# A list scheduler that counts a port shared by VectorE and GpSimd, and lets either take the low parts of weights

## The chip, the cores and the metric

The kernel runs on one core of one Trainium2 chip. The metric is device time in microseconds (us) for one execution, as the median of several; lower is better.

## The reference

A decay attention over 2 batches, 8 heads, 768 positions of width 64 feeds two feed-forward layers. The batch and head dimensions of its output are laid out as 1536 tokens by 512, and then:

```python
g = x @ w_gate                          # 512 x 1536
silu = g * (1.0 / (1.0 + np.exp(-g)))
val = x @ w_val
y = silu * val @ w_out                  # 1536 x 512: first MLP
h = y @ w_in                            # 512 x 2048
out = (h * np.cos(h)) @ w_out2          # 2048 x 512: second MLP
```

All weights come as 64-bit floats and are read as pairs of 32-bit words.

## The kernel before

Every large product is made of three fp32r matmuls (`mm3`, lines 142 to 147): high part of the weight by low part of the data, high by high, low by high. So every operand needs a high part (a copy on ScalarE) and a low part (a subtraction). One token block of 512 is a bank of the PSUM memory; eight banks circulate. Two of the three token blocks go through a seven-product scheme (products `b c a d 2 3 4`) that needs sums of weight pieces (`sa`, `sb` in the first MLP, `ta`, `tb` in the second) and of data pieces (the tiles `t1`, `t2`, `t3`).

The attention stage comes first (its code and order are not touched), with six first-MLP products in its last chunks. After it, all remaining work is given out by a list scheduler that runs while the kernel is built. Jobs are Python generators: each yields requests for an engine with a length in ns, or takes and gives buffers (`stock`: `s`, `g`, `y`, `ct`, `stage`, `ring`, `bank`). `run_all` picks what starts next by the lengths it believes in, emits the instruction, and so fixes one order for each engine. On the chip the engines keep that order and wait for each other by semaphores.

The jobs that matter here:

- `conv_job` turns one loaded weight piece into fp32: a scaling on ScalarE (`scale`, L189, tile `ct`), a shift (`shift`, L194, tile `raw`) and a merge (`join`, L201, `ct`) on VectorE. `split_job` then makes the high part `wh` on ScalarE and the low part `wl` on GpSimd (L638).
- `sums_job` makes two weight sums from two `ct` tiles in four half-size operations (128x256) on GpSimd.
- `turn_job` computes h*cos(h): ScalarE rounds, VectorE subtracts multiples of 2 pi twice (L921, tile `y`; L923, tile `s`), ScalarE takes absolute value and sine, VectorE multiplies. `finish` splits the result into `gh` (ScalarE) and `gl` (VectorE).
- `t_job` and `y_job` prepare `t1` to `t3` for the first and the second MLP with 128x1024 operations on VectorE; the tile they work in is named `sum`, their high parts go through ScalarE.
- `copy_job` copies product `b` or `c` from its bank to an `s` tile on ScalarE. Product `d` adds onto the bank of `c` and waits for that copy.
- `flush_job` adds a finished bank to a running `sum` on VectorE.

The scheduler's lengths for a 128x512 operation are 604 ns on VectorE and 1254 ns on GpSimd, whatever the other engine does. Data tiles in the "small" part of the weight ring are given up in `ring_down`, which makes room for the `s`, `g` and `y` tiles of the second MLP.

Of the kernel before, what the change touches and what calls it, by code (L numbers as in the profile page):

```python
# [45 lines left out]
def kernel(  # L46
# [463 lines left out]
    pieces = sorted(first_use, key=first_use.get)  # L510
    loads = [p for p in pieces if p[0] not in ("sa", "sb", "ta", "tb")]
    turned = min(seen[op] for op in downs[first2:]) - TURN

    mlp, live, ts, sums, where = {}, {}, {}, {}, {}
    f32 = lambda x: tuple(t.bitcast(F32) for t in x)
# [45 lines left out]
        "ct": [(0, i) for i in range(CT)], "stage": [], "ring": [],  # L561
    }
    wanted = {pool: [] for pool in stock}
    free_at = dict.fromkeys(("PE", "ACT", "DVE", "POOL"), 0)
    waiting = {e: [] for e in ("ACT", "DVE", "POOL")}
    n_jobs = [0]
    pe_units, pe_downs = [], []
# [59 lines left out]
        wanted[pool].remove(e)  # L627
        resume(e[2], t, i)

    def go(engine, ns, fn):  # L630

        return engine, ns, fn

    def tt(out, in0, in1, op, engine="DVE"):

        unit = nc.vector if engine == "DVE" else nc.gpsimd
        n = math.prod(out.shape[1:])
        return go(engine, n * (1.18 if engine == "DVE" else 2.45), lambda: unit.tensor_tensor(out=out, in0=in0, in1=in1, op=op))  # L638

    def act(out, src, fn, **kw):  # L640

# [3 lines left out]
    def either(out, in0, in1, op):  # L645

        n = math.prod(out.shape[1:])
        return "any", {"DVE": n * 1.18, "POOL": n * 2.45}, lambda e: (nc.vector if e == "DVE" else nc.gpsimd).tensor_tensor(
            out=out, in0=in0, in1=in1, op=op)

    def allowed(e, job, req):

# [2 lines left out]
    def run_all():  # L655

        while True:
            best = None
            for e in waiting:
                asks = [x for x in waiting[e] if allowed(e, *x)]  # L660
                if asks:
                    start = max(free_at[e], min(job.t for job, _ in asks))
                    if best is None or start < best[0]:
                        best = start, e
            op = next_pe()
            if op and (best is None or op[0] < best[0]):
                start, sub = op
                free_at["PE"] = start + sub["n"] * 227
                run_pe(sub, free_at["PE"])
                continue  # L670
            if best is None:
                assert not pe_units and not pe_downs and not blocked, (pe_units[:1], pe_downs[:1], blocked, wanted)
                return
            start, e = best
            job, req = min((x for x in waiting[e] if x[0].t <= start and allowed(e, *x)), key=lambda x: (x[0].prio, x[0].n))
            ns = req[1]
            if req[0] == "any":
                ns = ns[e]
                waiting["DVE"].remove((job, req))
                waiting["POOL"].remove((job, req))  # L680
                req[2](e)
            else:
                waiting[e].remove((job, req))
                req[2]()
            free_at[e] = start + ns
            resume(job, start + ns + LATENCY)

    unit_banks = set()
# [65 lines left out]

    def ring_job():

        for key in pieces[n_conv[0]:]:
            eligible = last_use[key] < turned
            if key[0] in ("sa", "ta"):
                other = ("sb" if key[0] == "sa" else "tb", key[1])  # L760
                got = []
                for k in (key, other):
                    i = yield "take", "ring", last_use[k] < turned
                    c = yield "take", "ct"
                    got.append((k, i, c))
                spawn(sums_job(got), first_use[key] - AHEAD, (yield "now",))
            elif key[0] not in ("sb", "tb"):
                yield "wait", ("load", key)
                i = yield "take", "ring", eligible
                c = yield "take", "ct"  # L770
                spawn(conv_job(key, i, c), first_use[key] - AHEAD, (yield "now",))
            granted.add(key)

    def split_job(key, i):

        wh, wl = ring_tiles(key, i)
        where[key] = i
        yield act(wh, fp[key], AF.Copy)
        yield tt(wl, fp[key], wh.bitcast(F32), ALU.subtract, "POOL")
        wsp[key] = (wh, wl)  # L780

    def conv_job(key, i, c):

        yield go("ACT", 550, lambda: scale(key, c))
        yield go("DVE", 455, lambda: shift(key))
        yield go("DVE", 610, lambda: join(key))
        now = yield "now",
        give("stage", stage_of.pop(key), now)
        signal(("fp", key), now)
        yield from split_job(key, i)  # L790
        now = yield "now",
        signal(("w", key), now)
        if key not in unsummed:
            give("ct", c, now)
        else:
            ct_of[key] = c

    def sums_job(got):

        which, f = got[0][0]  # L800
        rows = (("gate", f), ("val", f)) if which == "sa" else (("in2", f), ("in2", f + 1))
        for row in rows:
            yield "wait", ("fp", row)
        (a11, a12), (a21, a22) = ([fp[row][:, h * 256:h * 256 + 256] for h in range(2)] for row in rows)
        s = []
        for key, i, c in got:
            t = fp[key] = word_tile(c)
            s += [t[:, 0:256], t[:, 256:512]]
        yield tt(s[0], a21, a22, ALU.add, "POOL")
        yield tt(s[1], s[0], a11, ALU.subtract, "POOL")  # L810
        yield tt(s[2], a11, a21, ALU.subtract, "POOL")
        yield tt(s[3], a12, s[1], ALU.subtract, "POOL")
        for row in rows:
            unsummed.discard(row)
        for key, i, c in got:
            spawn(sum_split_job(key, i, c), first_use[key] - AHEAD, (yield "now",))
        for row in rows:
            yield "wait", ("w", row)
            if row in ct_of:
                give("ct", ct_of.pop(row), (yield "now",))  # L820
# [4 lines left out]
        signal(("w", key), (yield "now",))  # L825
        give("ct", c, (yield "now",))

    stage_of, ct_of, granted, last_load = {}, {}, set(), [0]
    unsummed = {(nm, f) for nm in ("gate", "val") for f in range(GROUP1, NF1)} | {("in2", f) for f in range(NF2)}

    def ring_down(t):

        small = range(RINGS[0], sum(RINGS[:2]))
        if "small" not in mlp or any(last_use[key] < turned and key not in granted for key in pieces[n_conv[0]:]):
            return
        if any(i in small for i in where.values()) or sum(i in small for _, i in stock["ring"]) < RINGS[1]:
            return
# [35 lines left out]
    def val_job(key, b, ps):  # L873

        yield "wait", ("s",) + key
        i, s = live.pop(key)
        yield tt(s, s, ps, ALU.mult)
        drop_bank(b, (yield "now",))
        yield from finish(key, i, s)

# [11 lines left out]
    def add_job(kind, f, nm, ps):  # L892
# [1 line left out]
        src, key = {"a": ("b", (0, f)), "2": ("d", (1, f)), "3": ("c", (1, f + (kind == "r")))}[nm]  # L894
        yield "wait", (kind, f, src)
        i, s = live[kind, f, src]
        yield tt(s, ps, s, ALU.add)
        signal((kind, f, nm), (yield "now",))
        key = ((0, 1)[kind == "r"],) + key
        if kind == "r":  # L900
            spawn(turn_job(key, s, lambda t: give("s", i, t)), seen[key] - EARLY, (yield "now",))
        elif nm != "3":
            yield act(s, s, AF.Silu)
            live[key] = i, s
# [5 lines left out]
            give("s", i, (yield "now",))  # L910
            yield from finish(key, j, s0)

    def turn_job(key, up, release):

        i = yield "take", "s"
        s = s_tile(i)
        n_ = s.bitcast(I32)
        yield act(n_, up, AF.Copy, scale=1.0 / (2.0 * math.pi))
        k = yield "take", "y"
        y = y_tile(k)  # L920
        yield go("DVE", 710, lambda: nc.vector.scalar_tensor_tensor(  # L921
            out=y, in0=n_, scalar=-TWO_PI_1, in1=up, op0=ALU.mult, op1=ALU.add))
        yield go("DVE", 610, lambda: nc.vector.scalar_tensor_tensor(  # L923
            out=s, in0=n_, scalar=-TWO_PI_2, in1=y, op0=ALU.mult, op1=ALU.add))
        give("y", k, (yield "now",))
        yield act(s, s, AF.Abs)
        yield go("ACT", 629, lambda: nc.scalar.activation(s, s, AF.Sin, scale=-1.0, bias=halfpi))
        yield tt(s, s, up, ALU.mult)
        release((yield "now",))
        yield from finish(key, i, s)  # L930

    def up_sub(op):
# [10 lines left out]
        def then(t):  # L943
            b, ps = held
            if nm == "in2":
                spawn(turn_job(key, ps, lambda t: drop_bank(b, t)), seen[key] - EARLY, t)
            else:
                spawn((gate_job if nm == "gate" else val_job)(key, b, ps), seen[op], t)
            if op == ("val", 1, GROUP1 - 1):
# [5 lines left out]
    def product_sub(op):  # L955
# [28 lines left out]
        def then(t):  # L984
# [4 lines left out]
            else:  # L989
# [2 lines left out]
                    spawn(val_job((0, 0, f), b, ps), seen[op], t)  # L992
                else:
                    key = (1, 0, f + 1)
                    spawn(turn_job(key, ps, lambda t: drop_bank(b, t)), seen[key] - EARLY, t)
            if kind == "q" and nm == "4" and f == NF1 - 1:
                signal("plain2", t)

# [39 lines left out]
    def flush_job(ph, blk, i, i_):  # L1038
# [10 lines left out]
        if first:  # L1049
            yield act(sm, ps, AF.Copy)  # L1050
        else:
            yield tt(sm, ps, sm, ALU.add)
        now = yield "now",
        give("bank", b, now)
        if last and ph == 0:
# [59 lines left out]
    with tc.manual_schedule():  # L1115
# [62 lines left out]
        stock["ct"] = [(0, i) for i in range(CT) if i not in ct_of.values()]  # L1178
        grow(1, mlp["small"])
        stock["ring"] = [(0, i) for i in free[n_conv[0]:]]  # L1180
        ahead = loads[n_conv[0]:n_loaded[0]]
        for n, key in enumerate(loads[:n_loaded[0]]):
            if key in ahead:
# [43 lines left out]
```

## Time and profile before

| | |
|---|---|
| median of 3 runs | 636.59 us (636.31 to 638.22) |
| the profiled execution, its own time | 636.19 us |
| its span, first to last instruction | 634.4 us |
| TensorE matmuls | 604.6 us busy, 95% of the span |
| VectorE | 475.7 us, 75% |
| ScalarE | 330.8 us, 52% |
| GpSimd | 248.1 us, 39% |
| DMA, mean over the span | 77 GB/s from and to HBM |

A busy share is a mean over stages that differ: the attention stage ends near 80 us, the first MLP near 380 us, and the second MLP takes the rest. Matmuls overlap in the pipeline, so that TensorE's own rate is read from the distance between the starts of two matmuls and not from the length of one.

### The profile page before, as it was taken

To read this page: it belongs to the slowest core of one execution; us is meant where nothing else is said; L and a number is where in the kernel's file an instruction comes from. 1 tells how busy PE (TensorE), PEld (TensorE's weight loads), DVE (VectorE), ACT (ScalarE), POOL (GpSimd) and SP (SyncE) were. 2 spreads that over 40 slices of the span, in tenths; PEclk is the share of its full clock that TensorE was granted. 3 is DMA by queue.
4 is the path that set the end of the run, shared out by engine and by line. 5 is a ranking of instruction groups with operands and counts; after the bars stand their busy time and mean duration, and the time that the engine had idled before them with its cause. 6 is when DMAs were issued, how large, how long until landed. Compare 5 with 4: busy or idle time off the path is not lost.

```text
span 634.4 us, 8339 instructions
## 1 busy us (share of the span) xinstructions
PE 604.6 (95%) x3093; PEld 490.3 (77%) x3093; DVE 475.7 (75%) x664; ACT 330.8 (52%) x570; POOL 248.1 (39%) x212
## 2 busy tenths in 40 slices
PE   8999999599999999999999989899889999999997
PEld 5888878477888887788888867688668788878886
DVE  4676569975545457665477899899998999998854
ACT  2353435556462534443532568787667575756630
POOL 3333356973544343442522136116342535161000
PEclk9999999799999999999999999799999999999999
DMA  9998222331221131122231012122312131100005
GB/s 186 210 247 191 67 68 69 125 105 43 92 67 66 39 95 66 68 67 63 72 100 33 1 53 80 33 68 66 101 33 91 42 92 42 67 1 1 0 2 199
DMA packets 65433, 49.31 MB, mean 78 GB/s; under 512 B 38760, under 2 KB 60272, under 8 KB 65392
## 3 DMA queue, kind: packets, MB, share of 16 engines
q1 hardware_dynamic: 65360, 48.77, 27.2%
q8 instruction: 24, 0.39, 0.3%
q14 instruction: 17, 0.14, 0.1%
q10 hardware_dynamic: 32, 0.01, 0.0%
HBM read 45.61 MB, written 3.15 MB: 77 GB/s over the span
## 4 chain that ended last, share of the span: by engine, by line
PE 58%; DVE 26%; issue 5%; ACT 5%; POOL 4%; DMA 1%; DVEq 0%; POOLq 0%; ACTq 0%
PE bank L145 13%; PE bank L146 12%; PE bank L147 12%; PE bank L1020 4%; PE bank L1019 4%; PE bank L1021 4%; DVE sum L638 4%; DVE s L638 4%; DVE s L923 4%; DVE gl L638 4%; DVE ct L201 3%; DVE y L921 3%; DVE raw L194 2%; POOL ct L638 2%; PE bank L406 2%
## 5 line engine op out<-in xcount | busy, mean ns | idle before, releaser
L638 POOL TENSOR_TENSOR wl<-ct,wh 128x512 fp32r<-128x512 f32 x98 | 147.4, 1516 | 256.6 <-ACT wh L643 213.1
L145 PE MATMUL bank<-xl,wh 128*128 128x512 f32 x336 | 134.1, 399 | 14.7 <-ACT s L643 8.9
L146 PE MATMUL bank<-xh,wh 128*128 128x512 f32 x336 | 132.0, 393 | 0.0
L147 PE MATMUL bank<-xh,wl 128*128 128x512 f32 x336 | 131.8, 392 | 0.0
L638 DVE TENSOR_TENSOR gl<-s,gh 128x512 fp32r<-128x512 f32 x81 | 71.5, 885 | 45.0 <-ACT gh L643 44.8
L643 ACT ACTIVATE wh<-ct 128x512 fp32r<-128x512 f32 x98 | 59.6, 627 | 64.5 <-DVE ct L201 53.2
L145 PEld LDWEIGHTS bank<-xl,wh 128*128 128x128 f32 x336 | 63.6, 189 | 33.7 <-ACT s L643 10.9
L643 ACT ACTIVATE s<-s 128x512 f32<-128x512 f32 (+1 forms) x92 | 57.5, 629 | 59.6 <-DVE s L923 32.1
L145 PE MATMUL bank<-wl,gh 128*128 128x512 f32 x192 | 75.6, 394 | 2.2 <-DVE sum L638 2.0
L643 ACT ACTIVATE gh<-s 128x512 fp32r<-128x512 f32 x81 | 50.5, 626 | 49.0 <-PE bank L1020 36.6
L638 DVE TENSOR_TENSOR sum<-bank,sum 128x512 f32<-128x512 f32 x100 | 64.7, 682 | 14.8 <-PE bank L147 7.7
L147 PE MATMUL bank<-wh,gl 128*128 128x512 f32 x192 | 75.2, 392 | 0.0
L146 PE MATMUL bank<-wh,gh 128*128 128x512 f32 x192 | 75.2, 392 | 0.0
L147 PEld LDWEIGHTS bank<-xh,wl 128*128 128x128 f32 x336 | 63.6, 189 | 13.5
L146 PEld LDWEIGHTS bank<-xh,wh 128*128 128x128 f32 x336 | 63.7, 190 | 12.4
L638 POOL TENSOR_TENSOR ct<-ct 128x256 f32<-128x256 f32 x72 | 69.7, 987 | 3.3 <-DVE ct L201 2.0
L643 ACT ACTIVATE s<-bank 128x512 f32<-128x512 f32 (+1 forms) x91 | 53.2, 588 | 28.8 <-PE bank L147 27.7
L201 DVE SCALAR_TENSOR_TENSOR ct<-ct,raw 128x512 int32<-128x512 int32 x68 | 56.2, 826 | 7.3 <-ACT ct L189 4.9
L1019 PE MATMUL bank<-gh,wl 128*128 128x512 f32 x144 | 56.1, 389 | 0.0
L638 DVE TENSOR_TENSOR s<-bank,s 128x512 f32<-128x512 f32 x54 | 36.9, 684 | 25.5 <-PE bank L147 24.1
L1021 PE MATMUL bank<-gl,wh 128*128 128x512 f32 x144 | 56.0, 389 | 0.0
L1020 PE MATMUL bank<-gh,wh 128*128 128x512 f32 x144 | 56.0, 389 | 0.0
(99 smaller groups left out, 946.0 us busy)
## 6 DMA issues: line engine op xcount, KB each, us to landing
raw<-in_moe_w_out_dram SPq DMA_DIRECT2D x28, 512.0 KB, 3.3
raw<-in_moe_w_in_dram SPq DMA_DIRECT2D x16, 512.0 KB, 3.8
raw<-in_moe_w_gate_dram SPq DMA_DIRECT2D x12, 512.0 KB, 3.5
raw<-in_moe_w_val_dram SPq DMA_DIRECT2D x12, 512.0 KB, 3.5
q<-in_q_dram SPq DMA_DIRECT2D x12, 256.0 KB, 4.9
k<-in_k_dram SPq DMA_DIRECT2D x12, 256.0 KB, 5.1
v<-in_v_dram SPq DMA_DIRECT2D x12, 256.0 KB, 5.9
out_dram<-sum SPq DMA_DIRECT2D x12, 256.0 KB, 2.1
```

Of the source, the lines that this page charges most:

```text
L145: nc.tensor.matmul(ps, wh, xl, start=first, stop=False, **kw)
L146: nc.tensor.matmul(ps, wh, xh, start=False, stop=False, **kw)
L147: nc.tensor.matmul(ps, wl, xh, start=False, stop=last, **kw)
L194: nc.vector.tensor_scalar(out=lo, in0=lo, scalar1=29, scalar2=None, op0=ALU.logical_shift_right)
L201: nc.vector.scalar_tensor_tensor(out=w, in0=w, scalar=3, in1=lo, op0=ALU.logical_shift_left, op1=ALU.bitwise_or)
L638: return go(engine, n * (1.18 if engine == "DVE" else 2.45), lambda: unit.tensor_tensor(out=out, in0=in0, in1=in1, op=op))
L643: return go("ACT", 40 + n * 0.94, lambda: nc.scalar.activation(out, src, fn, **kw))
L921: yield go("DVE", 710, lambda: nc.vector.scalar_tensor_tensor(out=y, in0=n_, scalar=-TWO_PI_1, in1=up, op0=ALU.mult, op1=ALU.add))
L923: yield go("DVE", 610, lambda: nc.vector.scalar_tensor_tensor(out=s, in0=n_, scalar=-TWO_PI_2, in1=y, op0=ALU.mult, op1=ALU.add))
L1019: nc.tensor.matmul(ps, lo[:, cs], gh, start=first, stop=False)
L1020: nc.tensor.matmul(ps, hi[:, cs], gh, start=False, stop=False)
L1021: nc.tensor.matmul(ps, hi[:, cs], gl, start=False, stop=last)
```

## The change

In the scheduler, a VectorE operation whose operands all lie in SBUF and any operation of GpSimd now hold one shared resource, `port`, for the length that the scheduler believes in; one that reads PSUM does not. The low parts of weights (`wl`) and the sums of weights, which went to GpSimd, become requests of kind `either`: VectorE may always take one, GpSimd only where VectorE is so long in its present instruction that GpSimd would end earlier. A request's earliest start is computed for each one apart, then priority decides. ScalarE, VectorE and GpSimd are taken to be free only some us after the start of the scheduled part; banks carry times at which they come free. The small ring tiles are used for a prefix of the pieces, so that they can be given up by count.

```diff
+    n_small = next(n for n, key in enumerate(pieces) if last_use[key] >= turned)
...
-    free_at = dict.fromkeys(("PE", "ACT", "DVE", "POOL"), 0)
+    free_at = {"PE": 0, "ACT": 2400, "DVE": 1800, "POOL": 4000, "port": 0}
...
-    def go(engine, ns, fn):
-        return engine, ns, fn
+    def go(engine, ns, fn, port=False):
+        return engine, ns, fn, port or engine == "POOL"
...
-                asks = [x for x in waiting[e] if allowed(e, *x)]
-                if asks:
-                    start = max(free_at[e], min(job.t for job, _ in asks))
-                    if best is None or start < best[0]:
-                        best = start, e
+                for job, req in waiting[e]:
+                    if not allowed(e, job, req):
+                        continue
+                    start = max(free_at[e], job.t, free_at["port"] if req[3] else 0)
+                    rank = max(start, free_at[e]), job.prio, job.n
+                    if best is None or rank < best[0]:
+                        best = rank, e, job, req
...
             free_at[e] = start + ns
+            if req[3]:
+                free_at["port"] = start + ns
...
-            eligible = last_use[key] < turned
+            eligible = n < n_small
...
-            granted.add(key)
+            granted[0] = n + 1
+            ring_down((yield "now",))
...
-        yield tt(wl, fp[key], wh.bitcast(F32), ALU.subtract, "POOL")
+        yield either(wl, fp[key], wh.bitcast(F32), ALU.subtract)
...
-        yield go("DVE", 455, lambda: shift(key))
-        yield go("DVE", 610, lambda: join(key))
+        yield go("DVE", 400, lambda: shift(key), True)
+        yield go("DVE", 610, lambda: join(key), True)
...
-        yield tt(s[0], a21, a22, ALU.add, "POOL")
-        yield tt(s[1], s[0], a11, ALU.subtract, "POOL")
-        yield tt(s[2], a11, a21, ALU.subtract, "POOL")
-        yield tt(s[3], a12, s[1], ALU.subtract, "POOL")
+        yield either(s[0], a21, a22, ALU.add)
+        yield either(s[1], s[0], a11, ALU.subtract)
+        yield either(s[2], a11, a21, ALU.subtract)
+        yield either(s[3], a12, s[1], ALU.subtract)
...
+        recent = [(turn_of["acc"] + j) % 4 for j in range(4)]
+        stock["bank"] = [(0, i) for i in range(4, 8)] + [(900 * j, i) for j, i in enumerate(recent)]
```

The new order follows from these rules. Two places show it. The first is ScalarE's queue where `t_job` of the first MLP ends; `xh_546<-sum` is its last high part, `s_1270` and `s_1280` (before: `s_1294` and `s_1310`) are the copies of products `b` and `c` that free the first seven-product group. Before:

```order
L643 ACTIVATE s_1294<-bank0_1287 128x512
L643 ACTIVATE wh_1299<-ct_1262 128x512
L643 ACTIVATE xh_546<-sum_1072 128x1024
L643 ACTIVATE s_1310<-bank1_1303 128x512
L643 ACTIVATE wh_1301<-ct_1263 128x512
```

With the change:

```order
L647 ACTIVATE s_1270<-bank1_1263 128x512
L647 ACTIVATE wh_1285<-ct_1173 128x512
L647 ACTIVATE s_1280<-bank4_1273 128x512
L647 ACTIVATE xh_546<-sum_1072 128x1024
L189 ACTIVATE ct_1308<-raw_1257 128x512
```

The copy of `c` stood behind the high part `xh_546` and now stands ahead of it.

The second is VectorE's queue in the second MLP, some 470 us into the trace of before: a conversion (`raw`, `ct`) among the operations of several `turn_job`s. Before, the low part of `ct_4200` is on GpSimd and so not here:

```order
L201 SCALAR_TENSOR_TENSOR ct_4200<-ct_4200,raw_4007 128x512
L638 TENSOR_TENSOR s_4161<-s_4161,s_4141 128x512
L921 SCALAR_TENSOR_TENSOR y_4212<-s_4199,s_4087 128x512
L923 SCALAR_TENSOR_TENSOR s_4199<-s_4199,y_4212 128x512
L638 TENSOR_TENSOR gl_4250<-s_4161,gh_4249 128x512
L921 SCALAR_TENSOR_TENSOR y_4256<-s_4226,bank5_4095 128x512
```

With the change, all on VectorE:

```order
L201 SCALAR_TENSOR_TENSOR ct_4198<-ct_4198,raw_4001 128x512
L929 SCALAR_TENSOR_TENSOR y_4220<-s_4191,s_4069 128x512
L640 TENSOR_TENSOR s_4096<-s_4096,s_4030 128x512
L652 TENSOR_TENSOR wl_4240<-ct_4198,wh_4239 128x512
L640 TENSOR_TENSOR s_4149<-s_4149,s_4124 128x512
L931 SCALAR_TENSOR_TENSOR s_4191<-s_4191,y_4220 128x512
L640 TENSOR_TENSOR gl_4246<-s_4096,gh_4245 128x512
```

The `wl` operation has moved into VectorE's queue, three places behind the merge that it follows, and waits there for `wh_4239` of ScalarE. Over the whole program 82 of the 98 scheduled `wl` operations and 52 of the 72 sums move to VectorE; 16 and 20 stay on GpSimd.

## Rows read from the trace of the kernel before

**Rows 1.** Stretches: length; busy us (x count) of PE, PEld, DVE, ACT, POOL; clock, DMA.

```profile
82.90:131.25 48.35, 41.58 (x170) 33.28 (x171) 42.50 (x43) 24.80 (x42) 38.64 (x25) 0.93 0.28 88
131.25:356.99 225.74, 222.98 (x980) 183.19 (x978) 138.76 (x188) 101.86 (x176) 93.20 (x85) 1.00 0.21 68
356.99:383.30 26.31, 23.88 (x102) 18.40 (x101) 24.47 (x30) 15.44 (x26) 8.67 (x5) 1.00 0.20 61
383.30:562.20 178.90, 168.72 (x721) 136.10 (x720) 166.79 (x233) 127.22 (x224) 73.29 (x55) 0.98 0.19 59
562.20:634.40 72.20, 68.48 (x301) 56.05 (x299) 52.48 (x80) 30.64 (x52) 6.10 (x4) 0.99 0.12 44
```

**Rows 2.** Waits of TensorE, longest in total first: us in total, times, longest.

```profile
PE bank L145 <- DVE s L638: 10.0, 7, 3.9
PE bank L145 <- ACT s L643: 8.9, 4, 5.5
```

**Rows 3.** Timeline, 99.6 to 119 us: start, length, instruction, idle before and its releaser.

```profile
99.68 0.39 PE L146 MATMUL bank<-xh,wh 128*128 128x512 f32 x1
...
111.47 0.39 PE L1021 MATMUL bank<-gl,wh 128*128 128x512 f32 x1
...
114.00 1.69 DVE L638 TENSOR_TENSOR sum<-sum,xl 128x1024 f32<-128x1024 f32 x1
...
115.72 1.06 ACT L643 ACTIVATE xh<-sum 128x1024 fp32r<-128x1024 f32 x1 [2.66 <-DVE sum L638]
...
116.68 0.58 ACT L643 ACTIVATE s<-bank 128x512 f32<-128x512 f32 x1
...
117.31 0.80 PE L145 MATMUL bank<-xl,wh 128*128 128x512 f32 x1 [5.45 <-ACT s L643]
...
118.33 0.63 PE L147 MATMUL bank<-xh,wl 128*128 128x512 f32 x1
...
118.76 0.63 PE L145 MATMUL bank<-xl,wh 128*128 128x512 f32 x1
```

**Rows 4.** Timeline, 395 to 400 us.

```profile
395.36 3.00 POOL L638 TENSOR_TENSOR wl<-ct,wh 128x512 fp32r<-128x512 f32 x2 [0.35 <-ACT wh L643]
395.47 1.76 DVE L638 TENSOR_TENSOR gl<-s,gh 128x512 fp32r<-128x512 f32 x1
...
397.16 1.75 DVE L638 TENSOR_TENSOR s<-s 128x512 f32<-128x512 f32 x1
398.82 0.68 DVE L638 TENSOR_TENSOR s<-bank,s 128x512 f32<-128x512 f32 x1
...
399.56 0.80 PE L145 MATMUL bank<-xl,wh 128*128 128x512 f32 x1 [3.86 <-DVE s L638]
```

**Rows 5.** Timelines of VectorE, from stretches near 101, 362 and 455 us.

```profile
101.63 0.42 DVE L194 TENSOR_SCALAR raw<-raw 128x512 int32<-128x512 int32 x1
...
362.31 1.22 DVE L638 TENSOR_TENSOR sum<-sum 128x1024 f32<-128x1024 f32 x1
...
453.55 1.53 DVE L194 TENSOR_SCALAR raw<-raw 128x512 int32<-128x512 int32 x1
455.00 0.68 DVE L638 TENSOR_TENSOR gl<-s,gh 128x512 fp32r<-128x512 f32 x1
455.60 0.68 DVE L201 SCALAR_TENSOR_TENSOR ct<-ct,raw 128x512 int32<-128x512 int32 x1
```

**Rows 6.** Timelines of GpSimd, from stretches near 428 and 439 us.

```profile
428.19 0.74 POOL L638 TENSOR_TENSOR ct<-ct 128x256 f32<-128x256 f32 x1 [1.29 <-DVE ct L201]
...
439.51 1.30 POOL L638 TENSOR_TENSOR wl<-ct,wh 128x512 fp32r<-128x512 f32 x1 [2.29 <-ACT wh L643]
```

**Rows 7.** Costliest groups, whole run: busy us, mean ns of one, idle before and its releasers.

```profile
L638 POOL TENSOR_TENSOR wl<-ct,wh 128x512 fp32r<-128x512 f32 x98 | 147.4, 1516 | 256.6 <-ACT wh L643 213.1
L638 DVE TENSOR_TENSOR gl<-s,gh 128x512 fp32r<-128x512 f32 x81 | 71.5, 885 | 45.0 <-ACT gh L643 44.8
L638 DVE TENSOR_TENSOR sum<-bank,sum 128x512 f32<-128x512 f32 x100 | 64.7, 682 | 14.8 <-PE bank L147 7.7
```

More of the change, by code (lines that the diff above doesn't have):

```diff
@@ L628, in give, with tt @@
         resume(e[2], t, i)
-    def go(engine, ns, fn):
-        return engine, ns, fn
-    def tt(out, in0, in1, op, engine="DVE"):
+    def go(engine, ns, fn, port=False):
+        return engine, ns, fn, port or engine == "POOL"
+    def tt(out, in0, in1, op, engine="DVE", psum=False):
         unit = nc.vector if engine == "DVE" else nc.gpsimd
         n = math.prod(out.shape[1:])
-        return go(engine, n * (1.18 if engine == "DVE" else 2.45), lambda: unit.tensor_tensor(out=out, in0=in0, in1=in1, op=op))
+        return go(
+            engine, n * (1.18 if engine == "DVE" else 2.45), lambda: unit.tensor_tensor(out=out, in0=in0, in1=in1, op=op),
+            not psum,
+        )
     def act(out, src, fn, **kw):
@@ L648, in either @@
         return "any", {"DVE": n * 1.18, "POOL": n * 2.45}, lambda e: (nc.vector if e == "DVE" else nc.gpsimd).tensor_tensor(
-            out=out, in0=in0, in1=in1, op=op)
+            out=out, in0=in0, in1=in1, op=op), True
     def allowed(e, job, req):
@@ L659, in run_all @@
             for e in waiting:
-                asks = [x for x in waiting[e] if allowed(e, *x)]
-                if asks:
-                    start = max(free_at[e], min(job.t for job, _ in asks))
-                    if best is None or start < best[0]:
-                        best = start, e
+                for job, req in waiting[e]:
[5 more added lines that the diff above has]
+                        best = rank, e, job, req
             op = next_pe()
-            if op and (best is None or op[0] < best[0]):
+            if op and (best is None or op[0] < best[0][0]):
                 start, sub = op
@@ L673, in run_all @@
                 return
-            start, e = best
-            job, req = min((x for x in waiting[e] if x[0].t <= start and allowed(e, *x)), key=lambda x: (x[0].prio, x[0].n))
+            (start, _, _), e, job, req = best
             ns = req[1]
@@ L755, in ring_job @@
     def ring_job():
-        for key in pieces[n_conv[0]:]:
-            eligible = last_use[key] < turned
+        for n, key in enumerate(pieces[n_conv[0]:], n_conv[0]):
+            eligible = n < n_small
             if key[0] in ("sa", "ta"):
@@ L762, in ring_job @@
                 for k in (key, other):
-                    i = yield "take", "ring", last_use[k] < turned
+                    i = yield "take", "ring", eligible
                     c = yield "take", "ct"
@@ L826, in sum_split_job @@
         give("ct", c, (yield "now",))
-    stage_of, ct_of, granted, last_load = {}, {}, set(), [0]
+    stage_of, ct_of, granted, last_load = {}, {}, [0], [0]
     unsummed = {(nm, f) for nm in ("gate", "val") for f in range(GROUP1, NF1)} | {("in2", f) for f in range(NF2)}
@@ L833, in ring_down @@
         small = range(RINGS[0], sum(RINGS[:2]))
-        if "small" not in mlp or any(last_use[key] < turned and key not in granted for key in pieces[n_conv[0]:]):
+        if "small" not in mlp or granted[0] < n_small:
             return
@@ L876, in val_job @@
         i, s = live.pop(key)
-        yield tt(s, s, ps, ALU.mult)
+        yield tt(s, s, ps, ALU.mult, psum=True)
         drop_bank(b, (yield "now",))
@@ L896, in add_job @@
         i, s = live[kind, f, src]
-        yield tt(s, ps, s, ALU.add)
+        yield tt(s, ps, s, ALU.add, psum=True)
         signal((kind, f, nm), (yield "now",))
@@ L900, in add_job @@
         if kind == "r":
-            spawn(turn_job(key, s, lambda t: give("s", i, t)), seen[key] - EARLY, (yield "now",))
+            spawn(turn_job(key, s, lambda t: give("s", i, t), False), seen[key] - EARLY, (yield "now",))
         elif nm != "3":
@@ L911, in add_job, with turn_job @@
             yield from finish(key, j, s0)
-    def turn_job(key, up, release):
+    def turn_job(key, up, release, psum):
         i = yield "take", "s"
@@ L920, in turn_job @@
         y = y_tile(k)
-        yield go("DVE", 710, lambda: nc.vector.scalar_tensor_tensor(
-            out=y, in0=n_, scalar=-TWO_PI_1, in1=up, op0=ALU.mult, op1=ALU.add))
         yield go("DVE", 610, lambda: nc.vector.scalar_tensor_tensor(
-            out=s, in0=n_, scalar=-TWO_PI_2, in1=y, op0=ALU.mult, op1=ALU.add))
+            out=y, in0=n_, scalar=-TWO_PI_1, in1=up, op0=ALU.mult, op1=ALU.add), not psum)
+        yield go("DVE", 610, lambda: nc.vector.scalar_tensor_tensor(
+            out=s, in0=n_, scalar=-TWO_PI_2, in1=y, op0=ALU.mult, op1=ALU.add), True)
         give("y", k, (yield "now",))
@@ L927, in turn_job @@
         yield go("ACT", 629, lambda: nc.scalar.activation(s, s, AF.Sin, scale=-1.0, bias=halfpi))
-        yield tt(s, s, up, ALU.mult)
+        yield tt(s, s, up, ALU.mult, psum=psum)
         release((yield "now",))
@@ L945, in then @@
             if nm == "in2":
-                spawn(turn_job(key, ps, lambda t: drop_bank(b, t)), seen[key] - EARLY, t)
+                spawn(turn_job(key, ps, lambda t: drop_bank(b, t), True), seen[key] - EARLY, t)
             else:
@@ L994, in then @@
                     key = (1, 0, f + 1)
-                    spawn(turn_job(key, ps, lambda t: drop_bank(b, t)), seen[key] - EARLY, t)
+                    spawn(turn_job(key, ps, lambda t: drop_bank(b, t), True), seen[key] - EARLY, t)
             if kind == "q" and nm == "4" and f == NF1 - 1:
@@ L1051, in flush_job @@
         else:
-            yield tt(sm, ps, sm, ALU.add)
+            yield tt(sm, ps, sm, ALU.add, psum=True)
         now = yield "now",
```

## The prediction

> **What bounds the kernel now.** I read the busy time by stretch first. The stretches are cut at fixed counts of matmuls, so that the same cuts can be made afterwards: A is the change-over from attention to the first MLP, B the rest of the first MLP, C the change-over to the second, D the second MLP while weights are still converted, E the end. In one run of 52 matmuls, from the start at 99.68 to that at 111.47 [rows 3], they follow each other at 11.79/52 = 0.227 us. At that rate TensorE needs 38.5 for the 170 matmuls of A, 221.7 for the 978 of B (the rows also count those that straddle a cut), 22.7 for the 100 of C and 163.2 for the 720 of D. The stretches last 48.35, 225.74, 26.31 and 178.90 [rows 1], so TensorE loses 9.8, 4.0, 3.6 and 15.7 us, together 33.1. In E it needs 68.0 of 72.20, and what is left is the last sums and the output. The 33.1 us are all that a better order can win.
>
> The waits say who is late: VectorE's additions and products, 10.0 us in seven waits, and ScalarE's copies, 8.9 in four [rows 2]. The two longest show the same cause. At 111.47 TensorE stops for a copy on ScalarE that stands behind the high part `xh`, which waited 2.66 us for VectorE's `sum`, an operation of 1.69 [rows 3]; the like takes 1.22 elsewhere [rows 5]. TensorE stands still for 5.6, and then its matmuls come every 0.43 (118.33 to 118.76), which with a granted clock of 0.93 in this stretch is the lower of the two clock levels. Some ten matmuls at 0.43 cost 2.0 more. At 395.5 VectorE's `gl` and `s` take 1.76 and 1.75 beside two `wl` of GpSimd, the addition behind them ends late and TensorE waits 3.86 [rows 4]; it starts again with a matmul of 0.80, the sign of the lower level, and the granted clock of D is 0.98 [rows 1].
>
> So the limit is VectorE, and what makes it late is GpSimd. A shift that takes 0.42 alone takes 1.53 beside a `wl`; free 128x512 operations follow each other at 0.60 (455.00 to 455.60), though each row lasts 0.68 [rows 5]. Over the run `gl`, with all operands in SBUF, has a mean of 885 ns; `sum<-bank,sum`, which reads PSUM, has 682 in spite of GpSimd [rows 7].
>
> **What the change moves, and its cost.** An instruction holds VectorE 0.08 less than its row lasts (0.68 against 0.60), so a shift costs 0.34 and a 128x1024 operation 1.14. A 128x256 sum on VectorE isn't in the trace: at least half of 0.60, that is 0.30, at most 0.60; on the line through 0.60 and 1.14 it is 0.33, which I take. On GpSimd a free `wl` takes 1.30 and a sum 0.74 [rows 6]. Counts come from the two programs' order, cut at the same matmuls.
>
> Stretch D. Before: 210 operations of 128x512 and 20 shifts, 126.0 + 6.8 = 132.8 us. VectorE was busy 166.79 [rows 1], so 34.0 are waiting inside instructions for GpSimd, whose 32 `wl` and 24 sums need 41.6 + 17.8 = 59.4: 0.57 us of VectorE for each us of GpSimd. After: 238 of 128x512, 22 shifts and 17 sums, 142.8 + 7.5 + 5.6 = 155.9; GpSimd keeps 8 `wl` and 7 sums, 15.6 us. At 0.57 these cost 8.9, and VectorE needs 164.8; if they only meet operations that read PSUM, they cost nothing, and it needs 155.9. The two bounds lie at TensorE's 163.2. The `wl` gives GpSimd's 1.30 and its collision for 0.60 on VectorE, so VectorE gains 2 to 11 us, and no more.
>
> The Trainium skill, page "SBUF — State Buffer", section "Who interferes with whom", says that a VectorE instruction with two SBUF inputs, and a GpSimd instruction that reads SBUF, exclude each other for a whole instruction, while a VectorE instruction with one SBUF input outside the two-port modes is not held up. The trace agrees: 885 against 682 ns, and a shift of 1.53. By this rule and perfect turns D would come to 155.9 for VectorE; by the row's ratio of 0.57 to 164.8. The rule also speaks against the move: a `wl` that GpSimd did beside a PSUM reader was free, and it now costs 0.60 of the tightest engine.
>
> VectorE is idle 178.9 - 166.8 = 12.1 us in D. With all of it kept, D ends at 168.0 to 176.9; with none, TensorE's 163.2 decides. I take 169.5, near the lower end, since the scheduler now puts GpSimd's few operations where VectorE reads PSUM, and its lengths (604 and 400 ns) are close to those of the rows (0.60 and 0.34), so waits stand where the order expects them. **D gains 9.4.**
>
> Stretch A. VectorE needs 13 x 1.14 + 23 x 0.60 + 9 x 0.34 = 31.7 before and is busy 42.50 [rows 1]; after, 13 x 1.14 + 29 x 0.60 + 7 x 0.34 + 5 x 0.33 = 36.3, with 3.5 us left on GpSimd instead of 28.4. At A's ratio, 10.8/28.4 = 0.38, this adds 1.3. That is 37.6 in TensorE's 38.5: full, but it fits. The copy of `c` now stands ahead of `xh`, so the 5.6 us wait loses its cause, and with it the 2.0 of slow clock. What is late next is the merge before the `wh` that precedes this copy; I leave 2.2 us of loss. **A gains 7.6**; with half of the wait left, and the clock with it, 3.8.
>
> Stretch C. VectorE needs 5 x 1.14 + 22 x 0.60 + 2 x 0.34 + 3 x 0.33 = 20.6 in TensorE's 22.7, was busy 24.47 [rows 1], and loses its collisions with 8.67 us of GpSimd. The sine work also begins some 50 matmuls earlier, since the small ring is given up sooner. **C gains 2.0** of its 3.6. In B VectorE's 138.76 of 225.74 leave room for what is added (45 x 0.60 + 27 x 0.33 + 2 x 0.34 = 36.6); the few waits there have each their own cause, I take **1.0** of 4.0 (0 to 4).
>
> Banks with times and the late start of the engines only change the order at the start of A and cost nothing by themselves. ScalarE, the loads and TensorE's counts are the same; ScalarE's 127.22 busy in D's 178.90 [rows 1] covers its share.
>
> The new wait: a `wl` in VectorE's queue waits for its `wh` from ScalarE. On GpSimd such waiting was 213.1 us and cost nothing [rows 7]; on VectorE everything behind it stands, products and `gl` first, and TensorE waits for those.
>
> **The sum.** 634.4 - (9.4 + 7.6 + 2.0 + 1.0) = 614.4 of span; with 636.19 - 634.4 = 1.8 around it, 616.2. The profiled execution lies 0.4 below the median, within the spread of the runs. I predict 616.
>
> **Rivals.**
>
> *VectorE becomes the bound.* For it: 155.9 to 164.8 us of work in 163.2, with 12.1 of idle time that an in-order queue may keep. Then D ends at 176.9 (gain 2.0), A keeps half its wait (3.8), C gains 1.0, B nothing: 634.4 - 6.8 + 1.8 = 629.4. Against it: idle time shrinks where the order fits the lengths.
>
> *Slower: the moved low parts block VectorE.* Like `wl`, `gl` follows ScalarE's high part, and VectorE waits 45.0 us for 81 of them, 0.56 each [rows 7]. The 28 `wl` of D would add 15.7 to 176.9 and make 192.6 (13.7 more than now), and the 9 of A 5.0, leaving A 2.6. With C's 1.0: 634.4 + 13.7 - 3.6 + 1.8 = 646.3. It decides from w = 0.29 us for each moved `wl`, where D's loss of 28w - 2.0 reaches the gains left in A and C, 7.6 - 9w + 1.0. Against it: two or three independent operations stand between merge and `wl`.
>
> *The change does not do what it says:* the chip doesn't keep the plan and VectorE exchanges collisions for added work, 34.0 for 23.1 + 8.9 in D, while A stops at another copy. Then it stays near 636.
>
> **How the numbers follow.** The likeliest case, 0.70, runs from 606 (5 of the 33.1 us lost remain: 634.4 - 28.1 + 1.8 = 608.1, and 2 for the prices) to 625 (D at 176.9, the rest as forecast: 616.2 + 7.4 = 623.6). VectorE the bound, 0.19, 625 to 632. No change, 0.04. Slower, 0.06. Below 606, 0.01. The range 606 to 630 takes in the first and most of the second. A measurement here tells 0.3%, 1.9 us, from no change: faster 0.90, same 0.04, slower 0.06.
>
> **What would show it.** Right: `gl`, `y`, `s` of VectorE at 0.68 nearly everywhere, a mean of `gl` under 720 ns; GpSimd under 60 us in A to D together; no wait of TensorE over 2.5 us and no lower clock behind one, 43 us or less for A's 170 matmuls, 172 or less for D's 720, with VectorE busy 155 to 165 of it. Wrong: waits of `wl` for `wh` on VectorE of more than 8 us in D, a TensorE wait over 3 us, or D over 176 us.

## The result and the profile after

The changed kernel takes 605.03 us (median; 604.58 to 605.91), against 636.45 for the kernel before in the same comparison: a ratio of 0.950, with a 95% interval of 0.948 to 0.952. Faster was forecast, at 616 us in a range of 606 to 630; the time lies just below the range.

The stretches, cut at the same matmuls as [rows 1]; columns as there:

```profile
81.88:122.00 40.12, 38.83 (x171) 31.84 (x170) 38.31 (x54) 23.30 (x39) 3.86 (x4) 1.00 0.25 79
122.00:343.68 221.68, 221.68 (x979) 183.62 (x978) 155.35 (x260) 103.02 (x176) 16.99 (x17) 1.00 0.23 74
343.68:367.70 24.02, 23.56 (x101) 18.54 (x100) 23.28 (x35) 16.62 (x28) 3.28 (x2) 1.00 0.02 6
367.70:530.90 163.20, 163.20 (x721) 135.13 (x720) 159.58 (x277) 128.16 (x226) 18.01 (x15) 1.00 0.24 75
530.90:602.80 71.90, 68.16 (x301) 56.12 (x299) 51.90 (x82) 29.47 (x49) 0.00 (x0) 0.99 0.12 44
```

A is shorter by 8.2 us, B by 4.1, C by 2.3, D by 15.7, E by 0.3, and A begins 1.0 earlier: together the 31.6 by which the span went from 634.4 to 602.8. In B and D TensorE is busy for the whole length of the stretch: there is nothing left to win there. TensorE's longest waits on what it needs in the MLPs, where [rows 2] had 10.0 and 8.9 us:

```profile
PE bank L145 <- DVE s L640: 1.3, 1, 1.3
...
PE bank L145 <- DVE t2l L640: 0.3, 1, 0.3
```

The place of [rows 3], now near 110 us:

```profile
108.10 1.22 DVE L640 TENSOR_TENSOR sum<-sum,xl 128x1024 f32<-128x1024 f32 x1
...
108.76 0.58 ACT L647 ACTIVATE s<-bank 128x512 f32<-128x512 f32 x1
...
109.36 1.06 ACT L647 ACTIVATE xh<-sum 128x1024 fp32r<-128x1024 f32 x1
...
110.44 0.39 PE L145 MATMUL bank<-xl,wh 128*128 128x512 f32 x1
...
113.25 0.50 PE L145 MATMUL bank<-t2l,wh 128*128 128x512 f32 x1 [1.29 <-DVE s L640]
```

`sum` is back at 1.22 from 1.69, the copy of `c` (108.76) is out before `xh`, and product `d` starts at 110.44 without a wait. The next wait, 1.29, is for an addition on VectorE, and the granted clock stays at the upper level: 1.00 in A, against 0.93.

The groups that answer to [rows 7]:

```profile
L640 DVE TENSOR_TENSOR gl<-s,gh 128x512 fp32r<-128x512 f32 x81 | 56.3, 698 | 28.6 <-ACT gh L647 28.5
...
L640 DVE TENSOR_TENSOR sum<-bank,sum 128x512 f32<-128x512 f32 x100 | 65.8, 688 | 13.4 <-PE bank L147 7.7
...
L652 DVE TENSOR_TENSOR wl<-ct,wh 128x512 fp32r<-128x512 f32 x82 | 56.0, 691 | 10.3 <-ACT wh L647 9.4
```

`gl` went from 885 to 698 ns, so collisions (a VectorE operation within SBUF held up beside one of GpSimd) are nearly gone, and VectorE is idle 10.3 us ahead of the 82 `wl`, 0.13 each. In D VectorE works 159.58 of 163.20 us and waits for hardly anything:

```profile
DVE s L640 <- PE bank L147: 1.8, 3, 1.3
DVE s L640 <- ACT s L935: 0.6, 1, 0.6
DVE gl L640 <- ACT gh L647: 0.2, 1, 0.2
```

Its idle time there fell from 12.1 to 3.6 us. That is the term on which the forecast turned, and the prediction had only argued how much of it would stay. All the signs that the prediction named for being right came (`gl` at 698 ns, GpSimd 42.1 us in A to D, no wait of TensorE over 1.3 us, A 40.12 and D 163.20 us), and none of those for being wrong; the forecast gain was too small all the same. The experiments ask whether collisions cost the time, or an order that doesn't know of them.

### The profile page after: what moved, and what is told of

The parts are those of the page before. It is cut to its first block, busy times and chain, and to the rows that moved or that the text cites. A ratio compares the mean times of both kernels' runs of the same rounds, so it can differ in the third digit from the quotient of the medians.

```text
span 602.8 us, 8216 instructions
## 1 busy us (share of the span) xinstructions
PE 595.0 (99%) x3093; PEld 489.4 (81%) x3093; DVE 478.4 (79%) x799; ACT 331.6 (55%) x570; POOL 70.3 (12%) x77
## 4 chain that ended last, share of the span: by engine, by line
PE 88%; DVE 8%; DMA 2%; issue 1%; ACT 1%; POOL 0%; DVEq 0%; POOLq 0%
PE bank L145 22%; PE bank L147 22%; PE bank L146 22%; PE bank L1027 5%; PE bank L1029 5%; PE bank L1028 5%; DVE sum L640 3%; PE bank L406 2%; PE bank L400 2%; PE bank L378 2%; PE bank L321 2%; PE bank L354 1%; DVE ct L201 1%; DMA down_d<-down 1%; DMA dmask<-down_d 1%
## 5 line engine op out<-in xcount | busy, mean ns | idle before, releaser
L145 PE MATMUL bank<-xl,wh 128*128 128x512 f32 x336 | 131.4, 391 | 0.1
L640 DVE TENSOR_TENSOR gl<-s,gh 128x512 fp32r<-128x512 f32 x81 | 56.3, 698 | 28.6 <-ACT gh L647 28.5
L652 DVE TENSOR_TENSOR wl<-ct,wh 128x512 fp32r<-128x512 f32 x82 | 56.0, 691 | 10.3 <-ACT wh L647 9.4
L201 DVE SCALAR_TENSOR_TENSOR ct<-ct,raw 128x512 int32<-128x512 int32 x68 | 46.7, 688 | 1.6
L189 ACT ACTIVATE ct<-raw 128x512 f32<-128x512 f32 x68 | 44.4, 661 | 5.1 <-DMA raw<-in_moe_w_val_dram 2.7
```

The lines of the kernel that those rows point to most:

```text
L145: nc.tensor.matmul(ps, wh, xl, start=first, stop=False, **kw)
L189: nc.scalar.activation(t, words[:, :, 1].bitcast(F32), AF.Prelu, scale=2.0 ** -112, alpha=2.0 ** 32)
L201: nc.vector.scalar_tensor_tensor(out=w, in0=w, scalar=3, in1=lo, op0=ALU.logical_shift_left, op1=ALU.bitwise_or)
```

## The experiments

Theory P: TensorE loses time where the scheduler's lengths are not those of the chip, since the order then makes engines wait for each other. Theory M: the collisions cost it, and only taking work off GpSimd helps. Others are named where they come in. Each run is compared with the kernel before on its own chip, and its ratio has a 95% interval of 0.0014 to 0.0024 to either side.

### Work moved, nothing counted

Against the kernel before, with the ring rule of the change (which is priced alone further down):

```diff
-        yield tt(wl, fp[key], wh.bitcast(F32), ALU.subtract, "POOL")
+        yield tt(wl, fp[key], wh.bitcast(F32), ALU.subtract)
-        yield tt(s[0], a21, a22, ALU.add, "POOL")
+        yield tt(s[0], a21, a22, ALU.add)
```

(and the other three sums alike). Expected:

> The kernel before with the low parts and the sums planned and run on VectorE, and the new ring rule, without which the plan does not close; no port is counted, as GpSimd has next to nothing. Theory P (TensorE loses where the plan's lengths are not those of the chip): 604 to 612 us, as VectorE's lengths are now true, with 157 us of VectorE work in stretch D's 163. Theory M (only the collisions with GpSimd cost): 604 to 610. Theory C (the count of the port is what brings it): 620 or more, as nothing counts it here.

Measured: 603.71 us, ratio 0.950, just below the ranges of P and M. With 98 `wl` and 72 sums on VectorE, A takes 39.03 and D 163.19:

```profile
82.96:121.99 39.03, 39.02 (x171) 31.91 (x172) 38.28 (x57) 23.03 (x39) 1.48 (x1) 1.00 0.27 86
...
366.93:530.12 163.19, 163.19 (x721) 135.19 (x720) 160.02 (x281) 125.31 (x219) 0.00 (x0) 1.00 0.23 73
```

So the count of the port is not needed when GpSimd has next to nothing to do; theory C falls. P and M both stand. Two of VectorE's lengths are still those of before here (710 ns for `y`, 455 for the shift, against 0.60 and 0.34 us in the rows), and this costs nothing that can be seen: not every wrong length matters.

### Port counted, nothing moved

Against the changed kernel:

```diff
-        yield either(wl, fp[key], wh.bitcast(F32), ALU.subtract)
+        yield tt(wl, fp[key], wh.bitcast(F32), ALU.subtract, "POOL")
-        yield either(s[0], a21, a22, ALU.add)
+        yield tt(s[0], a21, a22, ALU.add, "POOL")
```

> The changed kernel, but low parts and sums stay on GpSimd alone; the port is counted. Theory P: 606 to 616 us, since the plan takes turns and the port has room (about 85 us of VectorE's work in SBUF and 60 us of GpSimd's in D's 163). Theory M: 630 to 640, GpSimd is busy as before and collides. D over 172 us speaks for M, under 168 for P.

Measured: 603.54 us, ratio 0.950, below the range that P gave. The stretches A and D, then two groups:

```profile
81.81:120.34 38.53, 38.53 (x171) 31.92 (x170) 35.13 (x37) 21.34 (x35) 21.78 (x16) 1.00 0.26 82
...
366.55:529.75 163.20, 163.20 (x722) 135.23 (x720) 147.61 (x226) 125.72 (x220) 65.78 (x55) 1.00 0.23 74
```

```profile
L640 POOL TENSOR_TENSOR wl<-ct,wh 128x512 fp32r<-128x512 f32 x98 | 138.2, 1422 | 237.1 <-ACT wh L647 219.0
...
L640 DVE TENSOR_TENSOR gl<-s,gh 128x512 fp32r<-128x512 f32 x81 | 65.7, 812 | 38.0 <-ACT gh L647 37.6
```

GpSimd works 65.78 us in D, and collides: `gl` has a mean of 812 ns. VectorE's own work there can be estimated from the trace's 204 operations of 128x512 and 22 shifts, at 0.60 and 0.34 us: 129.9 us. So 17.7 of its 147.61 are collisions, 15.6 us of the stretch it is idle, and yet TensorE stands nowhere in D. Theory M falls: work need not leave GpSimd, and the collisions and idle time that are left cost nothing in this order.

### The same work, the port not counted

Against the kernel of the last run:

```diff
-        return engine, ns, fn, port or engine == "POOL"
+        return engine, ns, fn, False
```

(and `False` for `either`, which is still used for the low parts of the second MLP's input). All other edits of the change stay, with the shorter length of `turn_job`'s first VectorE operation (`y`, 610 for 710 ns), which stands among the lines left out of the diff of the change.

> The changed kernel with low parts and sums on GpSimd alone and no port counted; ring rule, late start, bank times, the shift's shorter length and the new choice of the next request stay. Theory P (the order must know how long things take): 622 to 635 us, as the order is again ignorant of the collisions. Theory S (the other edits make the order good): 603 to 608.

Measured: 636.50 us, ratio 1.000 (0.998 to 1.001), above the range that P gave. D, and the first of the waits of TensorE:

```profile
382.98:563.59 180.61, 169.38 (x722) 135.81 (x720) 165.75 (x230) 125.91 (x221) 79.07 (x57) 0.98 0.20 65
```

```profile
PE bank L145 <- DVE s L640: 11.5, 10, 2.7
PE bank L145 <- ACT s L647: 6.3, 3, 3.6
PE bank L145 <- ACT sum L647: 3.5, 1, 3.5
```

The operations are the same as in the run before, and all but one (a low part of the second MLP's input) are on the same engines; the count adds no wait to the program. The order alone is worth 5% of the time, some 32 us, and late start, bank times, the two shorter lengths and the choice of the next request give nothing without the count. Theory S falls.

The two runs don't say through what the order works, since it changes the collisions too. By the same estimate VectorE loses 33.5 us to them in D without the count (165.75 less 132.3 for 208 operations and 22 shifts), against 17.7 with it. So a rival is left here: that the count helps because it makes collisions fewer. The next experiment takes them all away.

### No collisions, but an order that does not know the work

Against the kernel before, `tt` issues to VectorE whatever engine the scheduler has in mind:

```diff
-        unit = nc.vector if engine == "DVE" else nc.gpsimd
+        unit = nc.vector
```

> The kernel before in its old order, planned as if GpSimd did the low parts and sums, but these are issued to VectorE at the places where the plan has them on GpSimd. No collisions are left, while the plan is untrue: it leaves out some 26 us of VectorE's work in D (159 in 163). Theory P: 615 to 632 us, TensorE waits again. Theory M: 604 to 610.

Measured: 618.72 us, ratio 0.974.

```profile
82.83:127.11 44.28, 40.82 (x170) 32.78 (x171) 43.06 (x67) 26.07 (x44) 1.48 (x1) 0.96 0.33 103
...
375.80:544.91 169.11, 165.30 (x721) 134.27 (x720) 162.17 (x284) 126.36 (x223) 0.00 (x0) 1.00 0.20 63
```

No collision is left in D, and VectorE's work is that of the first experiment, yet A takes 5.2 us more and D 5.9 more than there. The two kernels differ in the ring rule as well, which alone is worth 2.7 in D and 0.1 in A (below). Nearly half of the gain, 15.0 of 31.7 us, is lost to the order, as P has it, and at most some 2 of it to the ring rule. An untrue order costs without any collision; how much of what is won with the port counted comes from fewer collisions, no run separates.

### Wrong lengths

VectorE's lengths a fifth too short, in the changed kernel; a fifth too long, in a kernel that never chooses GpSimd:

```diff
-            engine, n * (1.18 if engine == "DVE" else 2.45), ...
+            engine, n * (0.95 if engine == "DVE" else 2.45), ...
```

```diff
-            engine, n * (1.18 if engine == "DVE" else 2.45), ...
+            engine, n * (1.416 if engine == "DVE" else 2.45), ...
```

(and the lengths of the other VectorE operations; the shift's in the second alone).

> The changed kernel with the scheduler's lengths of VectorE operations cut by a fifth (485 instead of 604 ns, 490 instead of 610); nearly all low parts and sums come to VectorE, so there are hardly any collisions. Theory P: 609 to 622 us, TensorE waits for VectorE again in A and D. Theory M (collisions alone cost): 603 to 606.

> All low parts and sums on VectorE, with the scheduler's lengths of VectorE a fifth too long (725 instead of 604 ns). No collisions. Theory P as stated (any untrue length costs): 612 to 630 us. Theory P' (only lengths that are too short cost, since an order made for a slower engine still holds for a faster one, and waits are no part of what is emitted): 602 to 608.

Measured: 626.46 us, ratio 0.984, and 617.09, ratio 0.970. Too short, stretch D:

```profile
376.14:551.97 175.83, 166.65 (x721) 134.15 (x720) 161.72 (x282) 124.00 (x219) 2.09 (x2) 1.00 0.21 66
```

Too long, stretches D and E:

```profile
367.96:537.57 169.61, 166.45 (x722) 134.27 (x721) 150.95 (x263) 116.43 (x205) 0.00 (x0) 1.00 0.21 66
537.57:615.27 77.70, 69.95 (x301) 55.66 (x299) 67.03 (x111) 41.84 (x70) 0.00 (x0) 1.00 0.15 55
```

Too short costs more than P had it (609 to 622): 23.2 us over the kernel that has nearly the same work and the lengths of the change (GpSimd never chosen, below). Too long costs as well, 13.8 us over that kernel: 6.2 in D, where VectorE is idle for 18.7, and 5.5 in E, which has 111 VectorE instructions against 85, while D has 263 against 291: work has been put off. P' falls; that such an order starts what matters too late is a reading of these counts, and was not tried by itself.

### Both free, not counted; and neither late start nor bank times

The changed kernel with the two lines of the count taken out, as above; and the changed kernel with

```diff
-    free_at = {"PE": 0, "ACT": 2400, "DVE": 1800, "POOL": 4000, "port": 0}
+    free_at = {"PE": 0, "ACT": 0, "DVE": 0, "POOL": 0, "port": 0}
...
-        recent = [(turn_of["acc"] + j) % 4 for j in range(4)]
-        stock["bank"] = [(0, i) for i in range(4, 8)] + [(900 * j, i) for j, i in enumerate(recent)]
```

> The changed kernel with its either requests but without the count of the port. GpSimd then gets 36 us of work in A and B and 17 us in D, against 21 and 18 in the changed kernel's rows. Theory P: 606 to 616 us, a loss in A, where GpSimd has 15 us uncounted, and 1 to 5 us in D. If the count matters only where GpSimd has much to do: 604 to 607.

> The changed kernel without the late start of the engines and without the bank times. Theory P: 604 to 609 us, a loss in stretch A alone, up to 4 us. Theory S: 612 or more.

Measured: 616.89 us, ratio 0.970, just above the range that P gave, and 605.65, ratio 0.951. The first, stretches A and D:

```profile
81.90:128.57 46.67, 41.37 (x172) 33.40 (x170) 45.00 (x51) 25.33 (x43) 23.29 (x16) 0.93 0.29 91
...
374.76:542.94 168.18, 164.47 (x721) 134.79 (x720) 164.49 (x271) 129.07 (x225) 21.84 (x20) 1.00 0.23 72
```

With GpSimd 21.84 us busy in D, against 18.01 in the changed kernel, not counting the port costs 5.0 there, and 6.6 in A, where it is 23.29 busy against 3.86: without the count GpSimd is also chosen more often. The second can't be told from the changed kernel in its time. In its trace the first cut comes 0.9 us later, at 82.79 instead of 81.88, behind a wait of TensorE of 0.8 for a product on VectorE. The other four kernels without the late start have this wait too, and none of those with it.

### The ring rule alone

The kernel before with `n_small`, `eligible = n < n_small` and the call of `ring_down` in `ring_job`.

> The kernel before with the new rule for the small ring tiles alone. Theories P and M: 630 to 638 us, collisions and the plan's lengths are as before. Theory R (the earlier release of the small ring is what brings it): under 622.

Measured: 633.17 us, ratio 0.996 (0.994 to 0.999). It brings some 2 us; D takes 176.21 instead of 178.90, the other stretches hardly change, and theory R falls.

### GpSimd never chosen

```diff
-        return e == "DVE" or req[0] != "any" or max(...) + req[1]["DVE"] > req[1]["POOL"]
+        return e == "DVE" or req[0] != "any" or False and max(...) + req[1]["DVE"] > req[1]["POOL"]
```

> The changed kernel with GpSimd never chosen for low parts and sums: 161 us of VectorE work in D's 163. Theory P: 603 to 607 us, no loss in D over 2 us. Rival V (VectorE becomes the bound when it is this full): D over 167 us, 608 or more.

Measured: 603.30 us, ratio 0.948.

```profile
82.20:121.51 39.31, 38.83 (x171) 31.83 (x170) 38.04 (x56) 22.54 (x38) 1.47 (x1) 1.00 0.26 81
...
343.19:365.92 22.73, 22.73 (x102) 18.70 (x100) 22.29 (x35) 16.80 (x28) 0.00 (x0) 1.00 0.02 8
365.92:529.36 163.44, 163.44 (x721) 135.06 (x720) 162.89 (x291) 127.16 (x223) 0.00 (x0) 1.00 0.24 75
```

VectorE works 162.89 of D's 163.44 us, and TensorE still stands nowhere: rival V, a full VectorE that holds TensorE up, falls, as VectorE is busy for all but 0.6 us of D. Beside the changed kernel on one chip:

> The changed kernel beside the next one on one chip: 604.5 to 606.

> GpSimd never chosen, beside the changed kernel on one chip: 603 to 604, 1 to 2 us under it, as stretch A loses less.

Measured: 605.64 us (605.58 to 607.33; ratio 0.953) and 603.28 (602.95 to 603.35; ratio 0.949). The simpler kernel is 2 us faster. In the traces of these two runs 0.8 of it is in A (40.12 and 39.33) and 2.0 in C (24.76 and 22.75), so more in C than was expected. That is as far as this goes: of the 33.1 us that TensorE lost from A to D, about 1 is left.

## Why the prediction was wrong

- *What bounds the kernel, and how much can be won:* right. The 33.1 us of TensorE's waits were the measure, and 30.3 came back from A to D (8.2 + 4.1 + 2.3 + 15.7), 1.0 more ahead of A and 0.3 in E.
- *D gains 9.4:* this is the step that failed; it measured 15.7, and with it D has 6.3 of the 11.6 us by which the span was forecast too long (614.4 against 602.8). VectorE's work was sized rightly, 159.58 within 155.9 to 164.8. But the prediction let VectorE's work and its idle time together set D's end, and took "169.5, near the lower end" of 168.0 to 176.9, the ends with all of the idle 12.1 us kept. At the 159.58 of work that were measured, this would have been 9.9 us idle. It fell to 3.6, and D ended at TensorE's own 163.20. Nor is idle time a price by itself: with GpSimd kept at work and the port counted, VectorE has 17.7 of collisions and 15.6 of idle time in D, and TensorE waits for nothing there.
- *What makes VectorE late is GpSimd:* half right. With collisions and an order that ignores them the time is 636.50 us; with collisions and an order that counts them, 603.54; without collisions but with an order that doesn't know the work, 618.72. The prediction put the cost on the collisions, counted what the move saves of them ("2 to 11 us, and no more"), and gave the count of the port no term of its own. It did expect the scheduler to put GpSimd's operations where VectorE reads PSUM, and that came (last section); what it didn't see is that this is enough without the move.
- *B gains 1.0:* 4.1, the second largest miss. The few waits were said to have "each their own cause". Counting the port on the same engines brings B from 225.45 to 221.68, so one and the same edit takes them all away.
- *A gains 7.6, C 2.0:* 8.2 and 2.3. The order of ScalarE's copies was read rightly, and the granted clock stayed at 1.00 with the wait gone.
- *Late start and bank times cost nothing by themselves:* they gain a little, as TensorE's wait of 0.8 us ahead of A goes with them; the time of the whole cannot be told apart.
- *VectorE as the bound; low parts that block it:* neither came, even with VectorE 162.89 us busy in 163.44. A `wl` waits 0.13 us on VectorE, not the 0.56 of `gl` before. `gl` was a bad stand-in: even at the places of the old order, with `wl` issued to VectorE unplanned, 98 of them waited 11.5 us, 0.12 each. The rule of the Trainium skill's page "SBUF — State Buffer", section "Who interferes with whom", agrees with the runs: where GpSimd kept its work, `gl` within SBUF had a mean of 812 ns, while `sum<-bank,sum`, which reads PSUM, had 688 in that run as in the changed kernel, and 682 before. Neither the bound by this rule (155.9) nor the row's ratio (164.8) set D's length: TensorE did.
- *The range:* its lower end left 5 of 33.1 us lost, and 2.8 remained. The end should have been the sum of all waits, since nothing in the rows said that any of them had to stay.

## What to carry to other kernels

Where a list scheduler fixes the order of in-order engines, first compare its lengths with the trace, for each kind of operation and for pairs that collide: VectorE's lengths wrong by a fifth cost 14 us (too long) and 23 us (too short) of 603 here, while the collisions that were left where the order counted the port cost nothing. Correcting the lengths, with the operations left where they are, gave as much as moving them. And where a change can remove the cause of all waits of the bounding engine, the sum of these waits belongs inside the forecast's range.

## What the runs showed of the hardware

VectorE could be kept at work nearly without a gap: 291 instructions in D with 162.89 of 163.44 us busy and no wait of TensorE.

What GpSimd costs VectorE depends on where the order puts it, though nothing in the program enforces turns. In D, by the estimate above, VectorE lost 33.5 us for 60.7 us of GpSimd's own work (33 operations of 128x512 at 1.30 and 24 sums at 0.74) without the count, 0.55 for each us; with the count 17.7 for 59.7 (34 and 21), 0.30. Before the change it was 0.57. The starts and ends in the two traces show why. Without the count 70 of VectorE's 151 operations within SBUF in D overlap with one of GpSimd, with it 47 of 147; the ones that read PSUM go the other way, from 23 of 79 to 44 of 79, and beside GpSimd they last 0.68 us as they do alone.
